# Two attention blocks on one core: a planned order of work made again with other paces and margins, and another end of the program

## The chip, the core and the metric

The kernel runs on one core of a Trainium2 chip. Five engines work from instruction queues of their own: TensorE (PE in the profile; PEld is its weight load), VectorE (DVE), ScalarE (ACT), GpSimd (POOL) and SyncE (SP, which only issues transfers here). They meet through semaphores. The metric is the device time of one execution in microseconds (us), the median of several. Three runs of the kernel before took 678.16, 677.42 and 678.11 us; the median is 678.11.

## The reference

Two independent blocks on inputs of 2048 rows by 512 columns, bfloat16, 32 heads of 16 columns. Block A is linear attention, block B is softmax attention; the two outputs stand side by side.

```python
def _A_ref(x, wqkv, wo):
    H = 32; Dh = D // H
    qkv = (lambda x, *d: x.transpose(*d))((x @ wqkv).reshape(B, S, 3, H, Dh), 2, 0, 3, 1, 4)
    phi = lambda t: jnp.where(t > 0, t + 1, jnp.exp(t)) + 1e-6
    pq, pk = phi(q), phi(k)
    kv = jnp.einsum("bhsd,bhse->bhde", pk, v)
    z = jnp.einsum("bhsd->bhd", pk)
    o = num / den
...
def _B_ref(x, wqkv, wo):
    scores = jnp.einsum("bhqd,bhkd->bhqk", q, k) * scale
    p = _softmax(scores, axis=-1)
    o = jnp.einsum("bhqk,bhkd->bhqd", p, v)
    return (lambda x, *d: x.transpose(*d))(o, 0, 2, 1, 3).reshape(B, S, D) @ wo
...
return jnp.concatenate([a, b], axis=-1)
```

Almost all the work is in B: 32 heads of 2048 x 2048 scores, each of which needs an exponential.

## The kernel before

**Tiles.** The scores of B are made in blocks of 128 keys by 512 queries of one head, transposed, so that a block is a 128 x 512 tile. The work is cut into 32 units (four groups of eight heads, four stretches of 512 queries, even or odd heads of the group); a unit is 64 blocks (16 key blocks for each of 4 heads), so there are 2048 blocks. Line 881 makes the scores (four blocks at once in the four row groups of TensorE).

**Two ways to the exponential.** ScalarE takes most blocks: line 1111 turns two or three blocks at once (a tile of 128 x 1024 or 128 x 1536, from the PSUM tile pS) into PT. The scores stand in two PSUM slots, one of three banks and one of two, which take turns; the third bank of the wide slot can be lent to the other way, and then the wide slot too holds two blocks. VectorE takes the other blocks, from the PSUM tile pD or from the lent bank: line 988 adds a bias and cuts at a maximum, and the result, read as bits, is an approximate exponential (DI). Four such blocks make a group, and line 1184 makes two shifted copies of the group (DJ) on GpSimd, or now and then on VectorE; while VectorE does one, GpSimd is held. The three parts are weighted by three copies of V. So a block on ScalarE costs one product with V (line 1245, into PSUM tile pPV) and a block on VectorE costs three.

**End of a unit.** When all products of a unit are in pPV, VectorE transposes it (line 1374, OT) and takes a reciprocal (1385), GpSimd multiplies (1379, XN), and after every second unit VectorE transposes XN into ON (1389). ON times the output weights is line 544; line 548 evicts the result into a piece of KV, and a store sends it to DRAM.

**The rest.** Projections of B for later groups (544, 664), all of block A (the exponentials of its phi are line 701, on ScalarE) and the output products are jobs that are put in between.

**What sets the order.** A planner, run when the program is built, writes the order of each engine's queue. It keeps a clock for each engine (`T`), takes at each step the instruction that can begin first by its own costs, and multiplies each cost by a pace of the engine (`PACE`). `DSH` is its cost for a shift on VectorE. A stage that stands behind a GpSimd stage of a job is offered `JM` later than GpSimd's end (line 527). `SEEDS` picks, for every 45 us of planned time, one of five settings of a few limits (`MODES`) and a small jitter of the jobs' due times. On the chip the engines don't follow the planned times, only the order; whoever is early waits at its semaphore.

**The last unit.** Its exponentials end with two ACTIVATEs of half the queries each (line 1031), and everything after them is done in halves: `last_half` transposes (1309), takes reciprocals (1310), multiplies (1311, one half on GpSimd, one on VectorE) and transposes into ON (1313). `last_tiles` ends the last four output tiles (three of the four products of each were made ahead): the matmuls of line 544, then an eviction by the engine named in line 1328, then a store that one queue issues (1333).

**A branch at the end.** The program checks the range of its denominators (631, 644, 645, the matmul 652 and the reduction 653 into FLG). Each engine then reads FLG (1606) and either jumps over a general softmax that follows in its queue, or runs it; here all jump. GpSimd first waits for all stores. `mark` (line 1608) puts a hint for this jump into the queues of TensorE, ScalarE and VectorE, 60 operations before each queue's end. Behind the jump the engines meet (line 315), and the program is over.

Of the kernel before, what the change touches and what calls it, by code (L numbers as in the profile page):

```python
# [247 lines left out]
def bass_concat_heads__linear_attn_block__softmax_full_mha__prompt_kernel(nc, A_x, A_wqkv, A_wo, B_x, B_wqkv, B_wo, out):  # L248
# [28 lines left out]
    SHL = ("pool", "pool")  # L277
    LM = 5.0
    FU = 0.6
    SEEDS = (0, 357, 103, 277, 20, 42, 55, 76, 197, 262, 78, 81, 233, 301, 371)  # L280
    SEG = 45.0
    JIT = 6.0
    DBAL = 1
# [1 line left out]
    LONE = 0.0  # L285
    MODES = ((0.8, 36, 0.7, 0.2, 9.0), (1.2, 36, 0.7, 0.2, 9.0), (0.8, 48, 0.9, 0.2, 10.5), (1.2, 28, 0.7, 0.1, 9.0), (1.0, 36, 0.55, 0.35, 8.0))
    LDA = 1
    JM = 0.8
    DSH = 0.45
    XNT = 0.63  # L290
    VVT = 0.69
    HINT = 60
    HQ = ("pe", "act", "dve")
    FW = 3.4
    UT = 0.6
    AE = 40.0
# [2 lines left out]
    XNP = 1  # L299
    VVP = 0  # L300
    POOLT = lambda w: 0.284 + w * 0.00082
    PACE = {"pe": 1.0, "act": 1.0, "dve": 1.03, "pool": 1.0, "dma": 1.0}
    TRACE = None


# [9 lines left out]
    with es:  # L315
# [153 lines left out]
        def vis(eng, en_):  # L469
            return en_ + TAIL[eng] + SEM  # L470
# [18 lines left out]
        class Job:  # L489
# [32 lines left out]
            def go(self, i, end, bk, bi):  # L522
                eng = self.stages[i][0]
                eng2, dur, fn = self.stages[i + 1]
                if getattr(fn, "buf", None) is not None:
                    lease(fn.buf, 1)
                push(eng2, end if eng2 == eng else vis(eng, end) + (JM if eng == "pool" else 0.0),
                     (CPRIO if i + 1 else self.prio) if eng2 == "pe" else (0 if eng2 == "act" or (i + 1 <= self.rel and self.bank) else min(self.prio, 2)), dur,
                     lambda st_, en_, fn=fn: (fn(bk), self.stage_done(i + 1, en_, bk, bi)), getattr(fn, "kind", "f"))

# [758 lines left out]
            pr = 1 if out_ >= mode()[1] or final else 4  # L1289
            return [(t_, *make(rounds[:n]), pr) for n in range(len(rounds), 0, -1)]  # L1290

        FB = {}
        ahead = [(tl, hb) for tl in range(4) for hb in range(3)]

        def last_half(h, t_):
# [22 lines left out]
        def last_tiles():  # L1318

            Gp, c, e_ = unit(LU)  # L1320
            k = 4 * Gp + c
            for tl in range(4):
                def mm(bk, tl=tl):
                    bk = FB[tl]
                    sch.add("pe", lambda e: mm4(e, f32v(bk), ON[:, k, tl * 128:(tl + 1) * 128], WOb[:, 3, :], False, True),
                            reads=on_keys(k)[4 * (tl // 2):4 * (tl // 2) + 4] + [("Wb", 2)], writes=[bk[3]], accum=("ps", tl))
                mm.kind = "v"
                ln = ("act", "act", "dve", "act")[tl]
                def fin(bk, tl=tl, ln=ln):
                    bk = FB[tl]  # L1330
                    sch.add(ln, lambda e: copy_to(ln, lambda: obf(tl), lambda bk: f32v(bk))(e, bk), reads=[bk[3]], writes=kst(tl))
                    t = 4 * c + tl
                    stores.append(sch.add(out_lanes[tl], lambda e: e.dma_start(out[0][t * 128:(t + 1) * 128, 512:1024], obf(tl)),
                                          reads=kst(tl), queue="act" if tl == 3 else "sp", force_signal=True))
                urgent2.append(Job([("pe", 0.22, mm), (ln, 0.6 if ln == "dve" else 0.48, fin)], [("onf", tl // 2), ("ps", tl)] +
                                   [("akv", 1, bl) for bl in range(2)], [(-1, ("st", c, tl))], bank=False))

# [264 lines left out]
        def run(queue, e):  # L1602
            got, loc = [], []
            def hook(e):
                e.wait_ge(sems["dve"], flag_op.count)
                got.append(e.value_load(FLG.bitcast(mybir.dt.int32), min_val=0))
            sch.emit_queue(queue, e, sems, hook=(flag_op.idx if queue == "pool" else len(sch.ops), hook),
                           mark=(HINT, lambda e: loc.append(e.mark_branch_hint_location())) if queue in HQ else None)
            with e.If(got[0] > FLAG_BITS):
                if loc:  # L1610
                    bass.BassInstruction(list(loc[0].bb.instructions)[-1]).branch_hint(loc[0])
# [53 lines left out]
```

## Time and profile before

| what | us |
|---|---|
| median of three runs | 678.11 |
| the profiled execution, whole | 678.51 |
| its span, first to last instruction | 676.8 |
| ScalarE busy in it | 659.0 |
| TensorE busy | 645.3 |
| VectorE busy | 593.4 |
| GpSimd busy | 590.5 |

The profile counts an engine as busy while one of its compute instructions runs; matmul ends are modelled. Rows of instruction groups read: line, engine, operation, tile written <- tiles read, shapes, count, then busy us and mean ns of one (longer than the pace in a full queue, since neighbours overlap), then the engine's idle time just before them and who ended it. A row of the timeline has the start and the length in us first. All times of the trace count from the span's start.

### The profile page before, as it was taken

What the parts mean: (1) busy time and instruction counts of PE and PEld (TensorE: products, weight loads), DVE (VectorE), ACT (ScalarE), POOL (GpSimd) and SP (SyncE); (2) the same over time, 40 slices, a digit from 0 to 9 for tenths busy, and PEclk for the clock granted to TensorE, in tenths of its full rate; (3) what the DMA queues carried; (4) which work ended last, traced back from release to release, by engine and by line L of the source; (5) the groups of instructions that cost most, each with busy time, mean ns of one, the idle gap of its engine ahead of it and who ended that gap; (6) DMA issues with size and microseconds to landing.
All of it is one profiled execution on the core that took longest, in us unless ns stands there. A gap on an engine that the chain in (4) does not pass through costs nothing.

```text
span 676.8 us, 19573 instructions
## 1 busy us (share of the span) xinstructions
PE 645.3 (95%) x8533; PEld 207.6 (31%) x8533; DVE 593.4 (88%) x973; ACT 659.0 (97%) x699; POOL 590.5 (87%) x369
## 2 busy tenths in 40 slices
PE   8999999999999999999999999999999999999996
PEld 4334322233333432222223333232222232222233
DVE  6987889988998999889898988989889898979993
ACT  5999999999999999999999999999999999999995
POOL 5699989998999898999999898898868999899893
PEclk9999999999999999999999999999989999999999
DMA  9401110111100021001011010211001000011001
GB/s 216 96 2 18 41 22 10 25 37 32 33 17 18 17 63 41 17 4 24 18 40 32 19 33 32 41 25 21 13 7 35 26 2 16 17 56 32 17 32 36
DMA packets 55418, 21.76 MB, mean 32 GB/s; under 512 B 45600, under 2 KB 55328, under 8 KB 55328
## 3 DMA queue, kind: packets, MB, share of 16 engines
q1 hardware_dynamic: 54128, 20.07, 13.2%
q8 instruction: 68, 1.11, 0.7%
q10 hardware_dynamic: 1200, 0.39, 0.2%
q14 instruction: 22, 0.18, 0.1%
HBM read 4.19 MB, written 4.19 MB: 12 GB/s over the span
## 4 chain that ended last, share of the span: by engine, by line
ACT 92%; PE 5%; DVE 1%; DMA 1%; issue 0%; ACTq 0%
ACT PT L1111 90%; ACT pD L701 2%; PE pS L881 2%; PE pPV L1245 1%; DMA xTb<-in_B_x_dram 1%; ACT pS L701 1%; PE pS L544 1%; PE pD L544 0%; PE pD L751 0%; PE pD L664 0%; DVE DI L988 0%; PE pS L573 0%; DVE OT L1309 0%; PE pD L573 0%; ACT KV L548 0%
## 5 line engine op out<-in xcount | busy, mean ns | idle before, releaser
L1111 ACT ACTIVATE PT<-pS 128x1024 f16<-128x1024 f32 (+1 forms) x659 | 649.2, 1326 | 4.1 <-PE pD L881 2.1
L1184 POOL TENSOR_SCALAR DJ<-DI 128x2048 int16<-128x2048 int16 x290 | 549.5, 1895 | 70.2 <-DVE DJ L1184 30.0
L988 DVE TENSOR_SCALAR DI<-pD 128x512 uint16<-128x512 f32 (+1 forms) x481 | 326.2, 695 | 36.5 <-PE pD L881 29.3
L881 PE MATMUL pS<-QT,KM 32*128 32x512 bf16 x1555 | 258.9, 385 | 20.8 <-ACT PT L1111 15.1
L1245 PE MATMUL pPV<-PT,VV 128*17 128x512 f16 (+1 forms) x1398 | 228.4, 379 | 0.0
L1245 PE MATMUL pPV<-DJ,VV 128*17 128x512 f16 (+1 forms) x1300 | 222.4, 379 | 0.0
L881 PE MATMUL pD<-QT,KM 32*128 32x512 bf16 x493 | 177.9, 385 | 0.2
L1245 PE MATMUL pPV<-DI,VV 128*17 128x512 f16 (+1 forms) x650 | 150.3, 380 | 0.7 <-DVE OT L1374 0.7
L881 PEld LDWEIGHTS pS<-QT,KM 32*128 32x128 bf16 x1555 | 64.3, 91 | 276.6 <-ACT PT L1111 238.3
L988 DVE TENSOR_SCALAR DI<-pS 128x512 uint16<-128x512 f32 x157 | 107.0, 681 | 3.8 <-PE pS L881 2.4
L1245 PEld LDWEIGHTS pPV<-DJ,VV 128*17 128x17 bf16 x1300 | 45.5, 88 | 44.1 <-issue 39.3
L1245 PEld LDWEIGHTS pPV<-PT,VV 128*17 128x17 bf16 x1398 | 46.3, 88 | 40.6 <-issue 35.9
L881 PEld LDWEIGHTS pD<-QT,KM 32*128 32x128 bf16 x493 | 42.0, 91 | 9.8 <-DVE DI L988 4.1
L1245 PEld LDWEIGHTS pPV<-DI,VV 128*17 128x17 bf16 x650 | 31.5, 88 | 23.3 <-issue 18.8
L1184 DVE TENSOR_SCALAR DJ<-DI 128x2048 int16<-128x2048 int16 x36 | 29.3, 815 | 0.0
L544 PE MATMUL pD<-Wa,xTa 128*32 128x256 bf16 x704 | 26.9, 274 | 0.3 <-DVE KV L702 0.3
L544 PE MATMUL pD<-xTb,Wb 128*32 128x512 bf16 x304 | 23.3, 383 | 0.0
L1374 DVE STREAM_TRANSPOSE OT<-pPV 128x512 f32<-128x512 f32 x31 | 21.9, 706 | 1.6 <-PE pPV L1245 1.6
L1379 POOL TENSOR_TENSOR XN<-OT,ZRA 128x256 bf16<-128x256 f32 x31 | 19.3, 622 | 3.6 <-DVE DJ L1184 2.5
L548 DVE CAST KV<-pD 128x512 bf16<-128x512 f32 x21 | 14.4, 686 | 5.8 <-PE pD L544 5.8
L701 ACT ACTIVATE pD<-pD 128x512 f32<-128x512 f32 x23 | 19.1, 829 | 0.3 <-DVE PQT L700 0.3
L544 PEld LDWEIGHTS pD<-Wa,xTa 128*32 128x32 bf16 x704 | 16.1, 96 | 9.6 <-issue 6.4
(117 smaller groups left out, 392.8 us busy)
## 6 DMA issues: line engine op xcount, KB each, us to landing
out_dram<-KV SPq DMA_DIRECT2D x31, 128.0 KB, 1.7
Wa<-in_A_wqkv_dram SPq DMA_DIRECT2D x3, 512.0 KB, 4.9
KM<-KR SPq DMA_DIRECT2D x96, 16.0 KB, 1.8
Wb<-in_B_wqkv_dram SPq DMA_DIRECT2D x2, 384.0 KB, 5.8
Wb<-in_B_wqkv_dram SPq DMA_DIRECT2D x1, 512.0 KB, 4.6
Wa<-in_A_wo_dram SPq DMA_DIRECT2D x1, 512.0 KB, 4.3
Wb<-in_B_wo_dram SPq DMA_DIRECT2D x1, 512.0 KB, 3.7
xTa<-in_A_x_dram SPq DMA_TRANSPOSE x24, 3.3
```

The source lines that it names most:

```text
L544: ins = e.matmul(out[32 * g:32 * g + 32], lhsT=lhsT[:, 32 * g:32 * g + 32], rhs=rhs, start=start, stop=stop, tile_position=(0, 32 * g))
L548: return lambda e, bk: (e.tensor_copy(out_fn(), in_fn(bk)) if lane == "dve" else e.activation(out_fn(), in_fn(bk), ACTF.Copy))
L701: ex = lambda bk: sch.add("act", lambda e: e.activation(x(bk), x(bk), ACTF.Exp), reads=[bk[3]], writes=[bk[3]])
L881: return e.matmul(dst, lhsT=KM[32 * g:32 * g + 32, Gp % 2, e_, j * 128:(j + 1) * 128], rhs=QT[32 * g:32 * g + 32, Gp % 2, c * 512:(c + 1) ...
L988: sch.add("dve", lambda e: e.tensor_scalar(DI.bitcast(U16)[:, buf, i * 512:(i + n) * 512], f32v(DBANK[bi], 512 * n), EB, IMAX, op0=ALU.add ...
L1111: sch.add("act", lambda e: e.activation(PT[:, row, c0:c0 + w], SCR[sl][:, 0:w], ACTF.Exp, scale=SC / ESC), reads=skeys(sl)[:len(bl)], writ ...
L1184: op = sch.add(ln, lambda e: e.tensor_scalar(J, I, 1.0, float(SH[k]), op0=ALU.mult, op1=ALU.add), reads=[("DI", buf, i) for i in range(n)] ...
L1245: sch.add("pe", lambda e: e.matmul(dst[32 * g:32 * g + 17, 0:n], lhsT=VV[:, Gp % 2, k, j, 17 * h:17 * h + 17], rhs=P[:, q0:q0 + n], start= ...
L1374: sch.add("dve", lambda e: e.transpose(OT[:, 0, :], PVb[:, 0:512]), reads=[("PV", g) for g in range(4)], writes=[("OT", 0)])
L1379: mul = f_op("pool" if XNP else "dve", lambda e: e.tensor_tensor(xn[:, :, 16 * e_:16 * e_ + 16], o[:, :, 0:16], zr.unsqueeze(2).broadcast_ ...
```

## The change

It changes numbers of the planner, so that the order of all queues is another one from the start on, and it changes the end of the program.

- The planner's pace of VectorE goes from 1.03 to 1.005, that of GpSimd from 1.0 to 1.01, and its cost of a shift on VectorE from 0.45 to 0.55.
- The margin behind a GpSimd stage, `JM`, goes from 0.8 to 0.3, and to 0.1 once all scores have been issued.
- The table of seeds is another.
- In the last four tiles ScalarE evicts two and VectorE two, where it was three and one. A tile that ScalarE evicted is stored from its own queue if it is one of the last two stores.
- Each engine except GpSimd waits, before its jump at the end, until the last two of these stores have landed.
- The hint for the jump stands 8 operations before the queue's end on TensorE and VectorE and 6 on ScalarE, where it was 60.

```diff
-    SEEDS = (0, 357, 103, 277, 20, 42, 55, 76, 197, 262, 78, 81, 233, 301, 371)
+    SEEDS = (0, 292, 16, 156, 16, 170, 160, 25, 137, 21, 137, 162, 330, 341, 350)
...
-    JM = 0.8
-    DSH = 0.45
+    JM = 0.3
+    DSH = 0.55
...
-    HINT = 60
-    HQ = ("pe", "act", "dve")
+    HINT = {"pe": 8, "act": 6, "dve": 8}
...
-    PACE = {"pe": 1.0, "act": 1.0, "dve": 1.03, "pool": 1.0, "dma": 1.0}
+    PACE = {"pe": 1.0, "act": 1.0, "dve": 1.005, "pool": 1.01, "dma": 1.0}
...
-                push(eng2, end if eng2 == eng else vis(eng, end) + (JM if eng == "pool" else 0.0),
+                push(eng2, end if eng2 == eng else vis(eng, end) + (0.0 if eng != "pool" else JM if cur_unit() is not None else 0.1),
...
-        FB = {}
+        FB, fins = {}, []
...
-                ln = ("act", "act", "dve", "act")[tl]
+                ln = ("act", "dve", "dve", "act")[tl]
...
-                                          reads=kst(tl), queue="act" if tl == 3 else "sp", force_signal=True))
+                                          reads=kst(tl), queue="act" if ln == "act" and len(fins) >= 2 else "sp", force_signal=True))
+                    fins.append(stores[-1])
...
+                if queue != "pool":
+                    for o in fins[2:]:
+                        e.wait_ge(sems[o.lane], 16 * o.count)
             sch.emit_queue(queue, e, sems, hook=(flag_op.idx if queue == "pool" else len(sch.ops), hook),
-                           mark=(HINT, lambda e: loc.append(e.mark_branch_hint_location())) if queue in HQ else None)
+                           mark=(HINT[queue], lambda e: loc.append(e.mark_branch_hint_location())) if queue in HINT else None)
```

Lines from 288 on stand one line earlier in the changed kernel up to the new line in `fin` (881 becomes 880, 1111 becomes 1110, and so on).

**ScalarE, the beginning.** The kernel before, from its first exponentials (PT<-pS) on:

```order
L1111 ACTIVATE PT<-pS 128x1024 x6
L1111 ACTIVATE PT<-pS 128x1536
L1111 ACTIVATE PT<-pS 128x1024 x21
L1111 ACTIVATE PT<-pS 128x1536
L1111 ACTIVATE PT<-pS 128x1024 x3
L1111 ACTIVATE PT<-pS 128x1536
```

And the changed kernel there:

```order
L1110 ACTIVATE PT<-pS 128x1024 x6
L1110 ACTIVATE PT<-pS 128x1536
L1110 ACTIVATE PT<-pS 128x1024 x3
L1110 ACTIVATE PT<-pS 128x1536
L1110 ACTIVATE PT<-pS 128x1024 x3
L1110 ACTIVATE PT<-pS 128x1536
L1110 ACTIVATE PT<-pS 128x1024 x19
```

Among the first 29 exponentials there are two of three blocks before and three now. Over the whole program the narrow ones stay 581 and the wide ones go from 78 to 80.

**VectorE, the end.** The kernel before, from the multiplication of one half of the last unit (1311) to the jump; the two rows of 1313 are the two halves' transposes, s_pool marks the one that waits for GpSimd's half:

```order
L1311 TENSOR_TENSOR XN<-OT,ZRA 128x8x16 [waits s_dve]
L1313 STREAM_TRANSPOSE ON<-XN 128x256 [waits s_dve]
L631 TENSOR_REDUCE ZRA<-ZRA 128x1 x2
L644 TENSOR_SCALAR BN<-ZRA 128x1 [waits s_dve]
L645 SCALAR_TENSOR_TENSOR BN<-ZRA,BN 128x1 [waits s_dve]
L1313 STREAM_TRANSPOSE ON<-XN 128x256 [waits s_pool]
L548 CAST KV<-pS 128x512 [waits s_d23,s_pe]
L653 TENSOR_REDUCE FLG<-pPV 1x1 [waits s_pe]
L1606 TENSOR_LOAD FLG [waits s_dve]
```

And the changed kernel:

```order
L1310 TENSOR_TENSOR XN<-OT,ZRA 128x8x16 [waits s_dve]
L1312 STREAM_TRANSPOSE ON<-XN 128x256 [waits s_dve]
L1611 BRANCH_PREFETCH_HINT
L1312 STREAM_TRANSPOSE ON<-XN 128x256 [waits s_pool]
L630 TENSOR_REDUCE ZRA<-ZRA 128x1 x2
L547 CAST KV<-pS 128x512 [waits s_d23,s_pe]
L643 TENSOR_SCALAR BN<-ZRA 128x1 [waits s_dve]
L547 CAST KV<-pS 128x512 [waits s_d22,s_pe]
L644 SCALAR_TENSOR_TENSOR BN<-ZRA,BN 128x1 [waits s_dve]
L652 TENSOR_REDUCE FLG<-pPV 1x1 [waits s_pe]
L1606 TENSOR_LOAD FLG [waits s_dve]
```

The transpose of GpSimd's half stands ahead of the range check now, a second eviction (s_d22 is the semaphore of that tile's store lane) has come to VectorE, and the hint stands just ahead of them.

**ScalarE, the end.** The kernel before, from the last two half exponentials to the jump:

```order
L1031 ACTIVATE PT<-pS 128x2x256 [waits s_pe]
L1031 ACTIVATE PT<-pS 128x2x256
L548 ACTIVATE KV<-pS 128x512 [waits s_d24,s_pe]
L1333 DMA out_dram<-KV 128x512 [waits s_act]
L548 ACTIVATE KV<-pD 128x512 [waits s_d21,s_pe]
L548 ACTIVATE KV<-pS 128x512 [waits s_d22,s_pe]
L1606 TENSOR_LOAD FLG [waits s_dve]
L1606 REGISTER_ALU
L1606 ISA
L1609 COMPARE_AND_BRANCH
```

And the changed kernel:

```order
L1030 ACTIVATE PT<-pS 128x2x256 [waits s_pe]
L1030 ACTIVATE PT<-pS 128x2x256
L547 ACTIVATE KV<-pS 128x512 [waits s_d24,s_pe]
L547 ACTIVATE KV<-pD 128x512 [waits s_d21,s_pe]
L1332 DMA out_dram<-KV 128x512 [waits s_act]
L1606 TENSOR_LOAD FLG [waits s_dve]
L1606 REGISTER_ALU
L1606 ISA
L1612 COMPARE_AND_BRANCH [waits s_d22,s_d21]
```

One eviction is gone, the store's issue stands behind the second eviction and no longer between two, and the jump waits for the landing of two stores.

## The prediction, made before the changed kernel ran

> **What bounds the kernel now.** I read the page first: busy time by engine and the chain that ended last.
>
> ```profile
> PE 645.3 (95%) x8533; PEld 207.6 (31%) x8533; DVE 593.4 (88%) x973; ACT 659.0 (97%) x699; POOL 590.5 (87%) x369
> ACT 92%; PE 5%; DVE 1%; DMA 1%; issue 0%; ACTq 0%
> ```
>
> ScalarE is busy for 659.0 of 676.8 us and holds 92% of the chain. TensorE's 95% is no second bound of the same rank: the rest of the chain is at the beginning and the end. So the second view is ScalarE's timeline, and of it every row that begins with idle time of 0.25 us and more between the first exponential and the last.
>
> ```profile
> 9.06 16.22 ACT L1111 ACTIVATE PT<-pS 128x1024 f16<-128x1024 f32 x17 [1.57 <-PE pS L881]
> 25.55 9.27 ACT L1111 ACTIVATE PT<-pS 128x1024 f16<-128x1024 f32 x10 [0.27 <-PE pS L881]
> 35.63 14.71 ACT L1111 ACTIVATE PT<-pS 128x1024 f16<-128x1024 f32 x15 [0.82 <-PE pD L881]
> 158.59 4.20 ACT L1111 ACTIVATE PT<-pS 128x1024 f16<-128x1024 f32 x4 [0.42 <-PE pD L881]
> 438.52 0.58 ACT L701 ACTIVATE pD<-pD 128x512 f32<-128x512 f32 x1 [0.29 <-DVE PQT L700]
> 503.06 1.02 ACT L1111 ACTIVATE PT<-pS 128x1024 f16<-128x1024 f32 x1 [0.37 <-PE pD L881]
> 504.53 34.75 ACT L1111 ACTIVATE PT<-pS 128x1024 f16<-128x1024 f32 x35 [0.45 <-PE pD L881]
> ```
>
> From 9.06 us on the idle times are 0.27 + 0.82 + 0.42 + 0.29 + 0.37 + 0.45 = 2.62 us in all. The two at 503 to 504.5 fall into this stretch, where the granted clock (the column behind the engines, 0.58) was low:
>
> ```profile
> 501.00:505.00 4.00, 4.00 (x31) 0.77 (x30) 2.59 (x5) 3.17 (x4) 3.71 (x2) 0.58 0.00 0
> ```
>
> So a better order of the middle can win 2.62 us at most, whatever it does for the other engines. The time is the exponentials' work on ScalarE, plus this, plus the end, which is the third view: the rows from ScalarE's last exponential to the program's last instruction.
>
> ```profile
> 665.87 1.40 ACT L1031 ACTIVATE PT<-pS 128x512 f16<-128x512 f32 x2
> 668.90 0.45 DVE L1313 STREAM_TRANSPOSE ON<-XN 128x256 bf16<-128x256 bf16 x1
> 668.31 0.40 POOL L1311 TENSOR_TENSOR XN<-OT,ZRA 128x128 bf16<-128x128 f32 x1 [2.04 <-DVE ZRA L1310]
> 669.69 0.44 DVE L1313 STREAM_TRANSPOSE ON<-XN 128x256 bf16<-128x256 bf16 x1
> 669.40 0.64 PE pS L544 x8
> 670.06 0.65 DVE L548 CAST KV<-pS 128x512 bf16<-128x512 f32 x1
> 670.06 0.60 ACT L548 ACTIVATE KV<-pS 128x512 bf16<-128x512 f32 x1 [2.79 <-PE pS L544]
> 670.69 0.39 ACTq L1333 DMA_DIRECT2D out_dram<-KV  x1
> 671.18 0.60 ACT L548 ACTIVATE KV<-pD 128x512 bf16<-128x512 f32 x1 [0.52 <-PE pS L544]
> 671.68 0.59 ACT L548 ACTIVATE KV<-pS 128x512 bf16<-128x512 f32 x1
> L1333 SPq DMA_DIRECT2D out_dram<-KV x3: 332/332/333, 670.7 to 672.3; - x3
> DMA to landing us min/median/max: 2.0/3.1/4.2
> out_dram<-KV SPq DMA_DIRECT2D x3, 128.0 KB, 4.0
> out_dram<-KV ACTq DMA_DIRECT2D x1, 128.0 KB, 2.2
> ```
>
> The exponentials end at 667.27 (665.87 + 1.40) and the span at 676.8, so the end lasts 9.5 us. The last eviction ends at 672.27 and the last store is issued at 672.3. The first two stores land after 2.0 and 2.2 us; the other two take 4.0 and 4.2 (the median 4.0 of SP's three and the maximum). The last lands near 676.3, when GpSimd's jump begins:
>
> ```profile
> L1609 DVEq COMPARE_BRANCH  x1: 84/84/84, 671.7 to 671.7; - x1
> L1609 PEldq COMPARE_BRANCH  x1: 409/409/409, 671.8 to 671.8; - x1
> L1609 ACTq COMPARE_BRANCH  x1: 68/68/68, 672.3 to 672.3; - x1
> L1609 POOLq COMPARE_BRANCH  x1: 53/53/53, 676.3 to 676.3; - x1
> L315 PEldq DRAIN  x1: 63/63/63, 672.3 to 672.3; - x1
> L315 ACTq DRAIN  x1: 81/81/81, 672.7 to 672.7; - x1
> L315 DVEq DRAIN  x1: 59/59/59, 675.1 to 675.1; - x1
> L315 POOLq DRAIN  x1: 50/50/50, 676.5 to 676.5; - x1
> ```
>
> A jump and the step behind it (line 315) are 0.5 us apart on TensorE, 0.4 on ScalarE, 0.2 on GpSimd, and 3.4 on VectorE: it had to wait for its instructions. And instructions were being fetched while the slow stores moved, in the window from 673 to 677 us:
>
> ```profile
> q14 instruction: 4, 0.03, 2.6%
> q8 instruction: 1, 0.02, 1.5%
> ```
>
> Shares are of 16 engines over that window: 4.1% of 16 x 3.8 us (673 to the span's end) is 2.5 us of fetching. Had all of it gone to one DMA engine, the stores' pieces on that engine came some 2 us late, which is what the last two stores take longer than the first two. I take this as the cause and price its failure below.
>
> **The change part by part, on ScalarE's path.**
>
> *Two more wide exponentials* (80 for 78; narrow ones 581 as before, 32 of line 701 as before). Two stretches of the chain, six exponentials each, the first with a wide one among them:
>
> ```profile
> 145.61 5.94 ACT PT L1111 x6
> 235.68 5.51 ACT PT L1111 x6
> ```
>
> A narrow one is 5.51 / 6 = 0.92 us, a wide one 0.92 + 0.43 = 1.35. Two more: +2.7 us. This is certain, for nothing covers work on the engine that is the bound. What it relieves lies beside it: 6 blocks fewer on VectorE, 12 fewer block shifts, so GpSimd has 5 whole shifts and 2 half ones less.
>
> ```profile
> L1184 POOL TENSOR_SCALAR DJ<-DI 128x2048 int16<-128x2048 int16 x288 | 547.4, 1901 | 70.0 <-DVE DJ L1184 30.0 <-DVE DI L988 18.7 <-DVE VV L681 2.1
> L1389 DVE STREAM_TRANSPOSE ON<-XN 128x512 bf16<-128x512 bf16 x15 | 10.5, 701 | 0.0
> ```
>
> That is 5 x 1.9 + 2 of about half as much = 11 us of an engine that idles for 70 already: nothing.
>
> *The beginning.* The 0.27 + 0.82 = 1.09 us of idle time before 36 us come from TensorE and VectorE, which are full there (of 18 us from 9 to 27, VectorE 17.87, TensorE 16.68, ScalarE 17.67):
>
> ```profile
> 9.00:27.00 18.00, 16.68 (x195) 6.59 (x192) 17.87 (x28) 17.67 (x19) 10.22 (x6) 1.00 0.93 205
> ```
>
> The new order gives ScalarE three wide ones where it had two, and so 0.43 us of work where it starved, and takes the same block from VectorE. The gain lies between 0 and 1.1; I take 0.5.
>
> *Paces and margins.* VectorE's work is now laid 2.5% closer and what stands behind GpSimd up to 0.5 us closer. Where the real engine is late, its queue stands still, TensorE's next scores wait for a bank, and ScalarE starves once more than the one exponential in hand (0.92 us) is lost. Before, none of the 15 transposes behind GpSimd (L1389 above, idle 0.0) waited at all, so some of the old margin was unused. Bounds: a gain of the remaining 2.62 - 1.09 = 1.5, a loss of 0.24 at each of the 15 places, 3.6 us. I take a loss of 0.5, nearer to the row without waits.
>
> *The end.* The second transpose of line 1313 began at 669.69 and its input from GpSimd was there at 668.71 (668.31 + 0.40); directly behind the first one it begins near 669.35, 0.35 us earlier. The last two tiles' matmuls then follow the first two's at once, ready about 670.6 (670.04 + 0.55). ScalarE evicts its second tile from there and VectorE its second after its first (670.06 + 0.65, a small check step, 0.65): both are done near 671.4, 0.9 earlier than 672.27, as one eviction is off ScalarE and its store's issue (0.39) no longer stands between. The last issue then is near 671.45. No engine jumps until the stores have landed, so the fetches of jumps are out of their way, and a store takes the first two's 2.0 to 2.2, with four at a time rather 2.3: landing at 673.75, for 676.3. Then the slowest jump, 0.5 and no longer GpSimd's 0.2: 0.3 back. In all -2.5 + 0.3 = -2.2. Queued behind the new waits is only the jump of each queue, and for that only the end of the program waits. Best: 2.0 for the landing and nothing for the jump, -2.8. Worst: below.
>
> [...]
>
> *Sum*, against the profiled execution's own 678.51: + 2.7 - 0.5 + 0.5 - 2.2 = + 0.5, so 679.0. The median run is 0.4 below that execution: **678.6 us**, no change that shows. The smallest change that a measurement of this kernel can tell from none is about 0.2%, 1.36 us: 676.75 to 679.47 is the same.
>
> **The rivals.**
>
> *All of the idle time is won back (faster).* The beginning gives 1.1, the stretch of low clock (0.37 + 0.45 = 0.82) comes where ScalarE doesn't feel it, the closer margins cost nothing, and the end gives 2.6: 678.1 + 2.7 - 1.1 - 0.8 - 2.6 = 676.3. For it: TensorE and VectorE are loaded less, and VectorE never waited at line 1389. Against it: everything has to go well, and a low clock of 3 to 4 us starves ScalarE wherever it falls on matmuls that feed it.
>
> *The jump comes late (slower).* A hint doesn't hold on one engine, and its fetch now begins only when the stores have landed, in the open. With VectorE's 3.4 for the 0.5: 2.9 more, the end is +0.7 for -2.2, and the time 678.6 + 2.9 = 681.5. It decides for "slower" once the jump costs 1.4 us or more. For it: VectorE's jump missed in the profile. Against it: two of three hints held, and the new ones stand nearer to the jump.
>
> *The margins were needed (slower).* GpSimd's row for XN stands behind a shift of 1.9 us; if GpSimd is half a shift late, VectorE's transpose behind it, now 0.5 us closer, holds up the blocks of line 988 behind it, and through the bank ScalarE. Each place beyond the one exponential in hand costs up to 1.9 - 0.9 = 1.0 us; four of the 15 at 0.9 are +3.6 for my +0.5, 681.7. It decides from 1.4 us of new idle time of ScalarE on. Against it: GpSimd idles 70 us and has 11 us less to do.
>
> *The fetches were not the cause (slower).* The last stores take 4.0 us for another reason. Then the end keeps only the earlier evictions, -0.9 + 0.3 = -0.6: 678.1 + 2.7 - 0.5 + 0.5 - 0.6 = 680.2.
>
> **How the numbers follow.** The forecast has 0.45 (the certain +2.7 against an end that is read off row by row), the faster rival 0.17, the late jump 0.10, the margins 0.16, the fetches 0.12. Slower is 0.10 + 0.16 + 0.12 = 0.38, same 0.45, faster 0.17. The range reaches from just below the faster rival, 676.0, to the dearest slower ones, 681.7; the forecast's own range is 676.8 to 680.
>
> **What would show it.** The exponentials' groups: 581 and 80, at 0.92 and 1.35. ScalarE's idle time between the first and the last exponential: about 2.6; above 4.5 the margins were needed, near 1 the faster rival holds. The last exponential should end near 670. From there to the end of the span: about 7.3 us, with evictions done 4.1 after it, all four stores landing in 2.0 to 2.4 us, no instruction fetch beside them but the hints', and the jumps within 0.5 us of the landing. I am wrong if the stores still take 4 us, if a jump takes more than 1.5, or if ScalarE's idle time moves by 2 us and more.

## The result, and the profile after

| | median us | runs | lowest to highest |
|---|---|---|---|
| before, in the same comparison | 677.64 | 5 | 676.46 to 678.16 |
| after | 679.66 | 5 | 679.25 to 681.71 |

The ratio is 1.0038 with a 95% interval of 1.0024 to 1.0052: the changed kernel is slower by 0.38%, some 2.6 us (the two medians alone differ by 2.0). The time lies within the forecast's own range (676.8 to 680), but 1.1 above its 678.6 and above the 679.47 up to which it called the kernels the same. What happened at the end of the program is the rival of the late jump, though the time it gave (681.5) was 1.8 too high. The profiled execution took 679.58 us, and its span is 677.8.

The page of the changed kernel, busy time by engine and the chain that ended last:

```profile
PE 646.0 (95%) x8520; PEld 208.0 (31%) x8520; DVE 589.1 (87%) x971; ACT 660.4 (97%) x700; POOL 578.0 (85%) x362
ACT 93%; PE 4%; DMA 1%; DVE 0%; issue 0%
```

Nothing here warns: ScalarE still carries the chain, VectorE and GpSimd have 4 and 12 us less to do. The groups of the exponentials show the 581 narrow and 80 wide ones that the change should bring:

```profile
L1110 ACT ACTIVATE PT<-pS 128x1024 f16<-128x1024 f32 x581 | 571.7, 1303 | 2.7 <-PE pS L880 1.6 <-PE pD L880 1.0
L1110 ACT ACTIVATE PT<-pS 128x1536 f16<-128x1536 f32 x80 | 136.1, 1702 | 0.0
```

ScalarE's timeline of the changed kernel, the rows that begin with idle time and the last exponentials (start and length in us):

```profile
8.65 34.00 ACT L1110 ACTIVATE PT<-pS 128x1024 f16<-128x1024 f32 x35 [1.57 <-PE pS L880]
43.67 19.89 ACT L1110 ACTIVATE PT<-pS 128x1024 f16<-128x1024 f32 x20 [1.02 <-PE pD L880]
...
665.77 1.40 ACT L1030 ACTIVATE PT<-pS 128x512 f16<-128x512 f32 x2
```

One idle time is left, 1.02 us at 43.67, for the 2.62 of before. The exponentials run from 8.65 to 667.17 (665.77 + 1.40), 658.5 us, and end at the same time as before (667.27), with two wide ones more.

So what was lost was lost behind 667.17. The timeline of the end, all engines:

```profile
669.94 0.60 ACT L547 ACTIVATE KV<-pS 128x512 bf16<-128x512 f32 x1 [2.77 <-PE pS L543]
670.40 0.68 DVE L547 CAST KV<-pS 128x512 bf16<-128x512 f32 x1
670.44 0.59 ACT L547 ACTIVATE KV<-pD 128x512 bf16<-128x512 f32 x1
670.45 1.30 SPq L1332 DMA_DIRECT2D out_dram<-KV  x3
671.06 0.38 ACTq L1332 DMA_DIRECT2D out_dram<-KV  x1
```

And the issues of the last stores with their time to landing, then the jumps (line 1612) and the step behind them (314), each by its line (duration, then first and last start):

```profile
L1332 SPq DMA_DIRECT2D out_dram<-KV x3: 332/428/451, 670.4 to 671.3; - x3
DMA to landing us min/median/max: 1.7/1.9/2.1
L1612 POOLq COMPARE_BRANCH  x1: 53/53/53, 673.4 to 673.4; - x1
L1612 ACTq COMPARE_BRANCH  x1: 68/68/68, 673.5 to 673.5; - x1
L1612 DVEq COMPARE_BRANCH  x1: 84/84/84, 673.5 to 673.5; - x1
L1612 PEldq COMPARE_BRANCH  x1: 3922/3922/3922, 673.6 to 673.6; - x1
L314 ACTq DRAIN  x1: 81/81/81, 674.0 to 674.0; - x1
L314 DVEq DRAIN  x1: 58/58/58, 676.8 to 676.8; - x1
L314 PEldq DRAIN  x1: 63/63/63, 677.5 to 677.5; - x1
```

Evictions are done at 671.08 (670.40 + 0.68) and the last store lands at 673.4 (671.3 + 2.1), where GpSimd jumps. That is 2.9 us earlier than the 676.3 of before. Then TensorE needs 3.9 us for its jump and VectorE 3.3 (673.5 to 676.8), with no other work on any engine: 4.1 us pass from the landing to TensorE's step behind the jump. The end lasts 10.66 us for 9.49 before.

### The profile page after: what moved, and what is told of

It is laid out like the page before. It is cut to its first block, busy times and chain, and to the rows that moved or that the text cites. A ratio compares the mean times of both kernels' runs of the same rounds, so it can differ in the third digit from the quotient of the medians.

```text
span 677.8 us, 19552 instructions
## 1 busy us (share of the span) xinstructions
PE 646.0 (95%) x8520; PEld 208.0 (31%) x8520; DVE 589.1 (87%) x971; ACT 660.4 (97%) x700; POOL 578.0 (85%) x362
## 4 chain that ended last, share of the span: by engine, by line
ACT 93%; PE 4%; DMA 1%; DVE 0%; issue 0%
ACT PT L1110 91%; ACT pD L700 2%; PE pS L880 1%; PE pPV L1244 1%; DMA xTb<-in_B_x_dram 1%; ACT pS L700 1%; PE pD L543 1%; PE pD L1244 0%; PE pS L543 0%; PE pD L663 0%; PE pS L572 0%; PE pD L572 0%; DVE OT L1308 0%; DVE KV L547 0%; DVE ON L1312 0%
## 5 line engine op out<-in xcount | busy, mean ns | idle before, releaser
L1183 POOL TENSOR_SCALAR DJ<-DI 128x2048 int16<-128x2048 int16 x283 | 537.1, 1898 | 82.0 <-DVE DJ L1183 32.8
L987 DVE TENSOR_SCALAR DI<-pD 128x512 uint16<-128x512 f32 (+1 forms) x476 | 322.5, 695 | 43.4 <-PE pD L880 34.4
L1244 PE MATMUL pPV<-DJ,VV 128*17 128x512 f16 (+1 forms) x1288 | 227.0, 379 | 0.0
L880 PE MATMUL pD<-QT,KM 32*128 32x512 bf16 x488 | 170.1, 384 | 0.1
L1244 PE MATMUL pPV<-DI,VV 128*17 128x512 f16 (+1 forms) x644 | 145.6, 379 | 0.2 <-DVE OT L1374 0.2
L1244 PEld LDWEIGHTS pPV<-PT,VV 128*17 128x17 bf16 x1404 | 48.7, 88 | 40.4 <-issue 34.8
L880 PEld LDWEIGHTS pD<-QT,KM 32*128 32x128 bf16 x488 | 40.3, 91 | 6.6 <-DVE DI L987 2.9
L543 PE MATMUL pD<-xTb,Wb 128*32 128x512 bf16 x384 | 29.4, 384 | 0.0
L680 POOL TENSOR_SCALAR VV<-VV 128x544 bf16<-128x544 bf16 x24 | 15.4, 645 | 1.5 <-DVE VV L670 0.2
```

The source lines that it names most:

```text
L543: ins = e.matmul(out[32 * g:32 * g + 32], lhsT=lhsT[:, 32 * g:32 * g + 32], rhs=rhs, start=start, stop=stop, tile_position=(0, 32 * g))
L680: cp = f_op(lane, lambda e, k=k: e.tensor_scalar(vv(k), vv(0), SW[k], 0.0, op0=ALU.mult, op1=ALU.add), [("VV", t, sl, 0) for t in ts] + [( ...
L880: return e.matmul(dst, lhsT=KM[32 * g:32 * g + 32, Gp % 2, e_, j * 128:(j + 1) * 128], rhs=QT[32 * g:32 * g + 32, Gp % 2, c * 512:(c + 1) ...
L987: sch.add("dve", lambda e: e.tensor_scalar(DI.bitcast(U16)[:, buf, i * 512:(i + n) * 512], f32v(DBANK[bi], 512 * n), EB, IMAX, op0=ALU.add ...
L1183: op = sch.add(ln, lambda e: e.tensor_scalar(J, I, 1.0, float(SH[k]), op0=ALU.mult, op1=ALU.add), reads=[("DI", buf, i) for i in range(n)] ...
L1244: sch.add("pe", lambda e: e.matmul(dst[32 * g:32 * g + 17, 0:n], lhsT=VV[:, Gp % 2, k, j, 17 * h:17 * h + 17], rhs=P[:, q0:q0 + n], start= ...
```

## The experiments

To compare kernels I use two numbers of each profile: the **stretch**, from the start of the first exponential to the end of the last, and the **end**, from there to the end of the span. What lies ahead of the first exponential scatters from execution to execution (last section) and is left out. The median of each experiment is from 9 to 12 runs beside runs of the kernel before (15 to 35 of them, medians 677.43 to 677.68); the first two rows are the five runs each of the result. A diff is against the changed kernel where the text says nothing else.

| kernel | stretch | end | sum | median | ratio to before, 95% |
|---|---|---|---|---|---|
| before | 658.22 | 9.49 | 667.71 | 677.64 | |
| after | 658.53 | 10.66 | 669.19 | 679.66 | 1.0038 [1.0024, 1.0052] |
| e1_hint60 | 658.55 | 9.96 | 668.51 | 679.49 | 1.0029 [1.0019, 1.0040] |
| e2_hint_early | 658.53 | 7.23 | 665.76 | 677.06 | 0.9991 [0.9981, 1.0001] |
| e3_no_wait | 658.42 | 10.33 | 668.75 | 679.47 | 1.0033 [1.0021, 1.0045] |
| e4_order_alone | 658.45 | 8.89 | 667.34 | 678.82 | 1.0015 [1.0004, 1.0026] |
| e5_end_alone | 657.13 | 11.03 | 668.16 | 678.85 | 1.0016 [1.0005, 1.0027] |
| e6_end_hint_early | 657.18 | 7.26 | 664.44 | 675.46 | 0.9965 [0.9953, 0.9977] |
| e7_hint_early_no_wait | 658.52 | 6.74 | 665.26 | 676.29 | 0.9980 [0.9971, 0.9990] |
| e8_before_hint120 | 657.13 | 9.39 | 666.52 | 678.14 | 1.0007 [0.9996, 1.0019] |
| e12_best | 657.08 | 6.76 | 663.84 | 675.37 | 0.9965 [0.9954, 0.9976] |

The order of before appears five times: four stretches are 657.1 to 657.2, and only the execution that I predicted from has 658.22. The low clock at 501 us, which that execution shows and the other four do not, is the difference. So the usual sum of the kernel before is about 657.1 + 9.5 = 666.6, and against it the sums give the measured ratios to within half a microsecond: after +2.6 (0.38%), e2_hint_early -0.8 (measured -0.09%, -0.6), e6_end_hint_early -2.2 (measured -0.35%, -2.4).

**The jumps: where the hint stands.** My theory after the result, A: TensorE's jump went from 0.5 us to 3.9 because its hint was moved from 60 operations ahead of the queue's end to 8. In the trace it stood 5.0 us ahead of the last page of instructions that I take for TensorE's before the change (662.8 and 667.8), and 0.4 after it (667.3 and 667.8); VectorE's stood behind the one that I take for its last in both kernels and missed in both (3.4 and 3.3 us). With TensorE's hint back at 60 its jump should be short again, with VectorE's still long. What a hint does with a page no trace shows; A is a guess from these starts. The rival, B: it is the wait, which holds each engine at the jump, that makes it slow.

```diff
-    HINT = {"pe": 8, "act": 6, "dve": 8}
+    HINT = {"pe": 60, "act": 60, "dve": 60}
```

> The changed kernel with all three hints 60 operations before the end, as before the change; the waits before the jump stay. [...] The end is then set by VectorE: about 0.8 us shorter, 678.9 against 679.7. [...] Rival C (the new positions are right and something else is slow): ScalarE, whose hint goes from 6 to 60, may miss too, same or slower.

Ratio 1.0029 [1.0019, 1.0040]. By line, in this kernel:

```profile
L1612 PEldq COMPARE_BRANCH  x1: 503/503/503, 674.3 to 674.3; - x1
L314 PEldq DRAIN  x1: 62/62/62, 674.9 to 674.9; - x1
L314 DVEq DRAIN  x1: 57/57/57, 677.6 to 677.6; - x1
```

TensorE's jump is back at 0.5 us with the wait in place; VectorE's, which had missed in the kernel before too, still takes 3.3 (674.3 to 677.6) and ends the program. So the end went from 10.66 to 9.96 only, and the median came out at 679.49 for the 678.9 that I expected.

```diff
-    HINT = {"pe": 8, "act": 6, "dve": 8}
+    HINT = {"pe": 60, "act": 6, "dve": 120}
```

> The changed kernel with the hint 60 operations before the end on TensorE, 120 on VectorE, 6 on ScalarE as it is. By theory A all three stand ahead of their engine's last fetch: all jumps take 0.5 us, and the program ends 0.8 us behind the landing instead of 4.4, so 3.5 us less than the changed kernel: 676.1, and 1.5 below the kernel before. [...] By a rival D (a hint too far ahead is lost) TensorE hits and VectorE misses: 678.9.

Ratio 0.9991 [0.9981, 1.0001], 677.06 us, 2.6 less than the changed kernel. The jumps of this kernel:

```profile
L1612 DVEq COMPARE_BRANCH  x1: 84/84/84, 673.9 to 673.9; - x1
L1612 PEldq COMPARE_BRANCH  x1: 502/502/502, 673.9 to 673.9; - x1
L314 PEldq DRAIN  x1: 64/64/64, 674.5 to 674.5; - x1
L314 DVEq DRAIN  x1: 35/35/35, 674.5 to 674.5; - x1
```

Nothing but two hints moved, all jumps take 0.6 us, and the end is 7.23, which is the 7.3 of the prediction. This shows that the position of the hints is the whole of the end's loss.

The rival has an experiment of its own, the changed kernel without the waits:

```diff
-                if queue != "pool":
-                    for o in fins[2:]:
-                        e.wait_ge(sems[o.lane], 16 * o.count)
```

> The changed kernel without the waits before the jump, hints as changed. By my theory the missed jumps (3.9 us on TensorE, 3.2 on VectorE) begin when FLG is read, about 673.0 instead of 673.55, and so end 0.5 us earlier, and their fetches meet only the last pieces of the stores: 679.1 against 679.7. If the collision of fetches with stores were dearer here, the last store would land 1 to 2 us later, at 675, still under the jump: the same 679.1. If the waits cost nothing: 679.7.

Ratio 1.0033 [1.0021, 1.0045]: no better. TensorE's jump takes as long without a wait (the jump and the step behind it of this kernel):

```profile
L1609 PEldq COMPARE_BRANCH  x1: 4102/4102/4102, 675.7 to 675.7; - x1
L314 PEldq DRAIN  x1: 63/63/63, 679.9 to 679.9; - x1
```

The waits don't make the jump slow (3.9 us with them, 4.1 without). And without them the four stores still land in 1.7 to 2.1 us.

**The two halves of the change.** First the new order with all of the old end:

```diff
-    HINT = {"pe": 8, "act": 6, "dve": 8}
+    HINT = {"pe": 60, "act": 60, "dve": 60}
...
-                push(eng2, end if eng2 == eng else vis(eng, end) + (0.0 if eng != "pool" else JM if cur_unit() is not None else 0.1),
+                push(eng2, end if eng2 == eng else vis(eng, end) + (0.0 if eng != "pool" else JM),
...
-                ln = ("act", "dve", "dve", "act")[tl]
+                ln = ("act", "act", "dve", "act")[tl]
...
-                                          reads=kst(tl), queue="act" if ln == "act" and len(fins) >= 2 else "sp", force_signal=True))
+                                          reads=kst(tl), queue="act" if tl == 3 else "sp", force_signal=True))
...
-                if queue != "pool":
-                    for o in fins[2:]:
-                        e.wait_ge(sems[o.lane], 16 * o.count)
```

> The changed order alone: paces, margin 0.3, shift cost and seeds of the change, but the whole end as before (evictions three and one, store queues, hints at 60, no waits). My account: the middle is 0.1 to 0.5 us shorter than before in spite of 2.7 us more work on ScalarE (idle time 1.0 for 2.6), and the end is that of the kernel before with its 9.5 us: 677.3, the same as before. If the margins or the two wide exponentials cost what my sum took (+2.7), 680.

Ratio 1.0015 [1.0004, 1.0026], some 1 us slower than before, where I had expected no difference. That expectation compared stretches with the one execution of before that held the low clock. The stretch is 658.45, like every kernel with this order (658.4 to 658.55), and so 1.3 longer than the usual 657.1; the end is 0.6 shorter than the profiled 9.49. The opposite, the kernel before with the whole new end and the margin of 0.1 behind the last scores (the diff is against the kernel before):

```diff
-    HINT = 60
-    HQ = ("pe", "act", "dve")
+    HINT = {"pe": 8, "act": 6, "dve": 8}
...
-                push(eng2, end if eng2 == eng else vis(eng, end) + (JM if eng == "pool" else 0.0),
+                push(eng2, end if eng2 == eng else vis(eng, end) + (0.0 if eng != "pool" else JM if cur_unit() is not None else 0.1),
...
-                ln = ("act", "act", "dve", "act")[tl]
+                ln = ("act", "dve", "dve", "act")[tl]
...
-                                          reads=kst(tl), queue="act" if tl == 3 else "sp", force_signal=True))
+                                          reads=kst(tl), queue="act" if ln == "act" and len(fins) >= 2 else "sp", force_signal=True))
...
+                if queue != "pool":
+                    for o in fins[2:]:
+                        e.wait_ge(sems[o.lane], 16 * o.count)
```

> The kernel before with the whole end of the change (evictions two and two, store queues, waits before the jump, hints 8, 6 and 8, margin 0.1 in the last stage), its order and paces otherwise kept. Theory A: TensorE's and VectorE's hints stand behind their last fetch again, both jumps miss, and the end lasts 10.6 us as in the changed kernel for 9.5: 1.1 more than before, 678.6. If hints 8 ahead hold in this order, 7.3 us of end and 675.3. ScalarE's lost time in the middle: 3.8 us as in the profile of before, if it belongs to the order; near 2.8 if the stretch of low clock at 501 us was a chance of that one execution.

Ratio 1.0016 [1.0005, 1.0027]. By itself each half costs about 1 us; together they cost 2.6. ScalarE's rows with idle time in this kernel are those of the kernel before without the two of the low clock:

```profile
8.95 16.17 ACT L1110 ACTIVATE PT<-pS 128x1024 f16<-128x1024 f32 x17 [1.62 <-PE pS L880]
25.39 9.27 ACT L1110 ACTIVATE PT<-pS 128x1024 f16<-128x1024 f32 x10 [0.27 <-PE pS L880]
35.48 14.71 ACT L1110 ACTIVATE PT<-pS 128x1024 f16<-128x1024 f32 x15 [0.82 <-PE pD L880]
158.43 4.20 ACT L1110 ACTIVATE PT<-pS 128x1024 f16<-128x1024 f32 x4 [0.42 <-PE pD L880]
438.37 0.58 ACT L700 ACTIVATE pD<-pD 128x512 f32<-128x512 f32 x1 [0.29 <-DVE PQT L699]
```

To see what the order costs I take the time by which each exponential ended later than in a full queue (there, the ends lie 0.917 us apart for a narrow one, 1.344 for a wide one, 0.491 for a tile of 512): 2.72 us in e5_end_alone, 1.43 in the changed kernel. The new order has 2 x 1.344 = 2.69 more work and 1.29 less lost time: +1.40, and the stretches differ by 658.53 - 657.13 = 1.40.

But the jumps of e5_end_alone hold a surprise:

```profile
L1612 PEldq COMPARE_BRANCH  x1: 488/488/488, 673.1 to 673.1; - x1
L314 DVEq DRAIN  x1: 59/59/59, 676.8 to 676.8; - x1
```

With the hint 8 operations before the end TensorE's jump takes 0.5 here, where it took 3.9 in the changed kernel. By theory A a hint must stand ahead of the last page of its queue. The starts in the trace, in us, where a page is one packet of kind instruction (16 KB on q8, which I take for TensorE's, or 8 KB on q14):

| kernel | TensorE: hint | last page fetch | jump | VectorE: hint | jump |
|---|---|---|---|---|---|
| before | 662.8 | 667.8 | 0.5 | 628.1 | 3.4 |
| e1_hint60 | 664.8 | 668.6 | 0.5 | 629.2 | 3.3 |
| e2_hint_early | 664.4 | 668.3 | 0.5 | 586.3 | 0.6 |
| e8_before_hint120 | 663.7 | 668.3 | 0.5 | 586.6 | 0.6 |
| after | 667.3 | 667.8 | 3.9 | 668.8 | 3.3 |
| e5_end_alone | 666.2 | 666.2, then 669.5 | 0.5 | 667.7 | 3.8 |

On VectorE hints near 586 held and those from 628 on did not; a page is fetched at 618 to 624 in these kernels (the trace has two instruction queues, q8 and q14, for five engines, so that this page of q14 is VectorE's is an inference). On TensorE hints 3.8 to 5.1 us ahead of the last fetch held; the one 0.4 ahead did not, nor did that of e3_no_wait, which stands 0.4 ahead too. In e5_end_alone the hint stood at the very fetch, and an extra page came at 669.5. Theory A doesn't cover it, and why this hint held stays open.

ScalarE's hint 6 operations before the end is no safe place either. In the changed kernel and in most others it held, with a page of q14 fetched behind it (663.5 and 664.6 in the changed kernel). In e11_seeds_before, one of the last three kernels below, no page of that queue came between the hint (671.4) and the jump, and ScalarE was through its jump after 2.8 us, where it takes 0.5 elsewhere:

```profile
L1612 ACTq COMPARE_BRANCH  x1: 68/68/68, 681.6 to 681.6; - x1
L314 ACTq DRAIN  x1: 99/99/99, 684.5 to 684.5; - x1
```

So in all the runs every hint that missed stood behind its engine's last fetch or 0.4 us ahead of it (which pages are VectorE's and which ScalarE's is the same inference). Of the hints that stood so, only TensorE's in e5_end_alone held. How far ahead is enough isn't shown: ScalarE's held 1.1 us ahead of a page, TensorE's missed at 0.4.

**The new end with hints that hold**, on the order of before:

```diff
-    HINT = {"pe": 8, "act": 6, "dve": 8}
+    HINT = {"pe": 60, "act": 60, "dve": 120}
```

> The same with hints 60 operations before the end on TensorE and ScalarE and 120 on VectorE. Theory A: all jumps 0.5 us, the end lasts 7.3 us: 2.2 less than before, 675.3. Its difference to the changed order with the same hints (677.06) tells what the new order is worth: by the two profiles' stretches from the first to the last exponential (658.2 and 658.5) this one is 0.3 faster; if the new order is better in most executions, slower.

(The diff is against e5_end_alone.) Ratio 0.9965 [0.9953, 0.9977], 675.46 us: 3.4 less than with the late hints, and 2.2 less than before. The end is 7.26, as expected.

**Do the waits help?** With the hints right, the changed kernel without the waits:

```diff
-    HINT = {"pe": 8, "act": 6, "dve": 8}
+    HINT = {"pe": 60, "act": 6, "dve": 120}
...
-                if queue != "pool":
-                    for o in fins[2:]:
-                        e.wait_ge(sems[o.lane], 16 * o.count)
```

> The changed kernel with early hints (60, 6, 120) and without the waits before the jump. If the waits only guard against fetches of missed jumps, they cost 0.3 us here (the other engines jump while the stores move, GpSimd alone behind them): 676.8 against 677.06. If hits too start fetches (of the pages behind the target) that hold up the stores, the last two land after 3 to 4 us and it is 1 to 2 us slower: 678 to 679.

Ratio 0.9980 [0.9971, 0.9990], and the end 6.74 for 7.23 with the waits: they cost about 0.5 us in the profile and save nothing. The time is below both that I had named (676.8, or 678 to 679): no fetch met the stores here (their data moved until 673.68, the first page behind the jumps came at 674.43).

**Were the fetches the cause of the slow stores?** In the kernel before I moved only VectorE's hint:

```diff
-                           mark=(HINT, lambda e: loc.append(e.mark_branch_hint_location())) if queue in HQ else None)
+                           mark=(120 if queue == "dve" else HINT, lambda e: loc.append(e.mark_branch_hint_location())) if queue in HQ else None)
```

> The kernel before with one number changed: VectorE's hint 120 operations before the end instead of 60. Theory (fetches of VectorE's missed jump held up the last two stores): VectorE's jump takes 0.5 us, no fetch of it lies beside the stores, they land after 2.0 to 2.2 us instead of 4.0 and 4.2, and the end is 1.9 us shorter: 675.6. Rival (the stores are slow for another reason, or the fetches behind a hit do the same): VectorE's jump is short and the time the same, 677.5.

Ratio 1.0007 [0.9996, 1.0019]: no change, where my theory had 675.6. By line, in this kernel:

```profile
L1609 DVEq COMPARE_BRANCH  x1: 84/84/84, 672.6 to 672.6; - x1
L315 DVEq DRAIN  x1: 34/34/34, 673.2 to 673.2; - x1
L1333 SPq DMA_DIRECT2D out_dram<-KV x3: 332/332/341, 671.7 to 673.2; - x3
DMA to landing us min/median/max: 2.0/3.0/4.1
```

VectorE's jump now takes 0.6 us, and the last stores still take up to 4.1. The four fetches of this kernel come after jumps that held; what they hold the trace doesn't show, only their times, queues and sizes. Their starts stand here beside the time in which the last stores' data moved:

| kernel | stores' data moving until | fetches at | slowest landing |
|---|---|---|---|
| before | 675.81 | 673.18, 673.37, 673.84, 674.62, 676.04 | 4.2 |
| e8_before_hint120 | 676.64 | 673.82, 674.24, 674.64, 675.27 | 4.1 |
| e4_order_alone | 676.23 | 676.15, 676.24, 676.27, 676.88, 679.08 | 2.0 |
| e7_hint_early_no_wait | 673.68 | 674.43, 674.58, 674.83, 674.90 | 2.1 |
| after | 673.07 | 673.85, 674.58, 674.60, 674.84, 677.36, 678.20 | 2.1 |

Where fetches come while the stores move, the slowest store takes 4.1 to 4.2; where they come behind (in e4_order_alone with the last 0.1 us of the data), 2.0 to 2.1. In e5_end_alone the one extra page at 669.5 falls among the stores, and the slowest takes 2.7; in e9_margin08, below, one small page does, and it takes 2.5. That holds with the waits and without them: e4_order_alone has the old end, the same queues for the stores and no waits, and its jumps come late enough by themselves. The single pieces of the stores show the same. A piece of 1 KB takes about 47 ns. Pieces of more than 100 ns are in these four executions alone: 11 in the kernel before, 13 in e8_before_hint120, 2 in e5_end_alone, 1 in e9_margin08. In the kernel before only 33 of the 576 pieces start later than 1.9 us behind the last issue, and they make the landing late; where the stores land in 2.0 to 2.1 us, none does. I take the cause as well supported, though no run moved the fetches alone.

**The best of both**: the order of before, the new end, early hints, no waits; that is e6_end_hint_early without the waits, and the diff is against it.

```diff
-                if queue != "pool":
-                    for o in fins[2:]:
-                        e.wait_ge(sems[o.lane], 16 * o.count)
```

> The order of the kernel before, the new end (evictions two and two, store queues), hints 60, 60 and 120, and no waits before the jump. From e6 (675.46) less what the waits cost in the changed order (677.06 to 676.29, 0.8): 674.7. If the jumps come early enough here for their fetches to meet the stores, as in the kernel before, the last stores take 4 us and it is 676.5 or more.

Ratio 0.9965 [0.9954, 0.9976], 675.37 us, the lowest median of all, though not the 674.7 that I expected; its interval is that of e6_end_hint_early, so here the waits can't be told from none in the medians (the ends are 7.26 with and 6.76 without). The landing and the jumps of this kernel:

```profile
L1332 SPq DMA_DIRECT2D out_dram<-KV x3: 332/424/441, 669.2 to 670.1; - x3
DMA to landing us min/median/max: 1.7/1.9/2.1
L1609 PEldq COMPARE_BRANCH  x1: 404/404/404, 671.8 to 671.8; - x1
L1609 POOLq COMPARE_BRANCH  x1: 53/53/53, 672.2 to 672.2; - x1
L314 DVEq DRAIN  x1: 36/36/36, 672.4 to 672.4; - x1
```

TensorE and VectorE jump without a wait, just as the last of the stores' data has moved (671.85). The first fetch behind their jumps comes at 672.7, after the landing at 672.2, and by 672.4 every engine is through.

**Which number of the planner?** Three kernels, one execution each, turn back one number of the change alone (all with the hints of e2_hint_early):

```diff
-    JM = 0.3
+    JM = 0.8
```

> The changed kernel with the margin behind GpSimd at 0.8 as before, seeds not searched again, early hints (60, 6, 120). The planner then gives ScalarE 93 wide and 564 narrow exponentials, 1.9 us more work than the changed order. If the smaller margin costs ScalarE idle time, its lost time (1.43 us in the changed order) falls here below 1; if it costs nothing, it stays between 1.4 and 3, and the stretch from the first to the last exponential is 660.4 or longer.

```diff
-    PACE = {"pe": 1.0, "act": 1.0, "dve": 1.005, "pool": 1.01, "dma": 1.0}
+    PACE = {"pe": 1.0, "act": 1.0, "dve": 1.03, "pool": 1.0, "dma": 1.0}
```

> The changed kernel with the paces of before (VectorE 1.03, GpSimd 1.0), seeds not searched again, early hints. ScalarE gets 99 wide and 562 narrow exponentials, 7.7 us more work. If VectorE's closer pace is what leaves less lost time, it is near 2.7 here, as in the order of before; if the lost time is a matter of the table of seeds, anything from 1 to 5. The stretch of exponentials is 666 to 669.

```diff
-    SEEDS = (0, 292, 16, 156, 16, 170, 160, 25, 137, 21, 137, 162, 330, 341, 350)
+    SEEDS = (0, 357, 103, 277, 20, 42, 55, 76, 197, 262, 78, 81, 233, 301, 371)
```

> The changed kernel with the table of seeds of before, early hints. ScalarE gets 110 wide and 541 narrow exponentials, 3.6 us more work than the changed order. If the search was what held the work down, the stretch is 662 or longer (658.5 + 3.6) with a lost time like the changed order's; if the paces alone make a good order, it would be no longer than 659.

They took 681.16, 693.65 and 686.54 us, the stretches 661.2, 673.3 and 666.4. They tell little about margin or pace, for each changed the amount of work too: the wide exponentials of the three are 93, 99 and 110, with 564, 562 and 541 narrow ones. The lost time is 2.3, about 9 and 5.7 us: the first lies where I had it for a margin that costs nothing, the other two, which hold low clocks, above what I had named. In the last two TensorE's clock also fell to half again and again. One such place of e10_pace_before, by windows (sum of the stretch, busy time of the engines, then the granted clock):

```profile
343.00:353.00 10.00, 10.00 (x86) 2.18 (x81) 7.53 (x12) 8.53 (x10) 8.13 (x5) 0.72 0.13 26
```

ScalarE starves there (8.53 of 10 us). What the three do show: each of them has a stretch 2.7 to 14.8 us longer than the changed kernel's 658.5, so no one of these numbers, turned back alone, makes a better order here. Whether the smaller margin or the pace lowered the lost time in the new order (1.43 for 2.72) stays open.

## Which steps of the prediction held, and which failed

- **ScalarE as the bound**: right. The differences in stretch and end alone give the measured ratios.
- **Two more wide exponentials, +2.7**: right (2.69).
- **The beginning, -0.5, and the paces and margins, +0.5**: the two together were -1.3 (lost time 1.43 for 2.72), where the sum had them at nothing. The idle 0.27 and 0.82 before 36 us went, as hoped, and 1.02 came at 43.67 instead; but the places at 158 and 438 us are gone, and the smaller margins brought no new one. The transposes behind GpSimd still never wait in the changed kernel:

```profile
L1389 DVE STREAM_TRANSPOSE ON<-XN 128x512 bf16<-128x512 bf16 x15 | 10.5, 700 | 0.0
```

  The rival of the needed margins fell with it. "Idle about 2.6" was wrong: it is 1.02, the sign that was set down for the faster rival, whose account of the middle of the program came nearer than the forecast's. With that, the low clock and an earlier start, the last exponential ended at 667.17 and not near 670.
- **The sum was made against the profiled execution**, whose stretch was 658.22 - 657.13 = 1.1 us longer than usual for its order, by the low clock. I took 0.4 off for the median, 0.7 too little. The 0.82 of idle time at 503 to 504.5 was nothing that a change of order could win from the median run.
- **The end, evictions 0.9 earlier and stores landing at 673.75**: right. Done at 671.08 and landed at 673.4, in 1.7 to 2.1 us, with no fetch beside them. The rival "the fetches were not the cause" fell. (The 2.5 us of fetching in the profile of before are 2.65: the shares are of the window's whole 4.0 us, not of 3.8.)
- **"Then the slowest jump, 0.5"**: this step failed. It was 4.1 from landing to step, 3.6 more than I had. The end came out 1.2 longer than before instead of 2.2 shorter. I had noted that the new hints "stand nearer to the jump" as an argument for them; nearer is what broke TensorE's (3.9 us with the hint at 8, 0.5 with it at 60 in e1_hint60), and VectorE's, which had missed from 60 operations ahead, missed again. The waits then put both misses into the open, which in the kernel before had been covered: VectorE was through at 675.1 while GpSimd waited for the stores until 676.3.
- **The rival of the late jump** had the right event and price (2.9 more for VectorE's 3.4). Its 681.5 was too high by 1.8, since it stood on the same middle, which came out cheaper. It deserved more than 0.10: the profile showed one miss among three hints, and nothing in it said that a hint nearer to the jump would hold where a farther one had not.
- **That 679.66 still lies in the forecast's range is luck.** The jumps put some 3.4 us on the end that the sum did not have; the middle (1.3) and the low clock in the baseline (0.7) took 2.0 off it.

In all the runs a jump whose hint did not hold took 3.3 to 4.1 us on TensorE and VectorE (2.8 on ScalarE in e11_seeds_before), and one whose hint held 0.4 to 0.6.

## What to carry to other kernels

A hint that stood closer to its jump was not safer here: on TensorE those 3.8 to 5.1 us ahead of the last page held and those 0.4 ahead missed. Place it well ahead, and check each engine's jump in the trace for itself, after every change of the order too. Before you make every engine wait for the last transfer, look at which of them has slow work behind that wait which was hidden so far. And a forecast made against one execution needs a second one: a chance event in it, here 3.4 us of low clock, is otherwise counted as something that the change can win.

## What the runs showed of the hardware that was not expected

- **Pages come behind jumps that held, too.** Three of 8 KB and one of 16 KB come behind the jumps even where every hint held, as in e7_hint_early_no_wait; with one miss, in the kernel before, there are four and one, with two, in the changed kernel, four and two. Where they came beside the stores of 128 KB, in the kernel before and in e8_before_hint120, the slowest store landed after 4.2 and 4.1 us for the 2.0 to 2.1 where they came behind the stores, while the pages there took 0.3 to 1.0 us each in the trace.
- **The clock fell to half for 3.4 us** at 501 us in one of the five executions of the old order, and cost ScalarE about 1 us. In its one execution e11_seeds_before had three such stretches, and e10_pace_before was at half clock for some 17 us in all.
- **The start scatters.** The first exponential began at 8.65 to 9.40 us in nine profiles and at 11.07 to 11.44 in five (e3_no_wait, e4_order_alone, e8_before_hint120, e9_margin08, e10_pace_before), whatever the change. The load of x is not what differs: the first matmul on it starts at 5.8 to 6.6 us in the nine and at 6.4 to 6.6 in the five. From there to the first exponential it takes 2.8 to 3.4 us in the nine and 4.4 to 4.9 in the five, for the same matmuls run at about half the pace (eight of one projection into pD take 0.87 us in the kernel before, 1.71 in e3_no_wait). The trace's record of the granted clock begins, at full, between 4.9 and 7.2 us in the nine and between 10.0 and 11.0 in the five, so the late start goes with a later record of the full clock; what was granted ahead of it, and why the start differs, no run here shows. The executions with the late start were 681.94 and 680.63 us in kernels whose medians are 679.47 and 678.82. The two of five runs of the changed kernel that took 681.5 and 681.7 may be of this kind; their traces were not taken.
